# Window attention and FFN on one core: the first batch's mask on PE, values paired on VectorE, loads and stores rearranged

## The chip, the cores and the metric

The kernel runs on one core of a Trainium2 chip. The metric is the device time in microseconds; the times of the kernel before are eight runs. A profiled execution of the same kernel gives the trace that the text reads. In its tables PE is TensorE's matmuls, PEld its weight loads, DVE is VectorE, ACT is ScalarE, POOL is GpSimd, and SP is SyncE, which issues most loads. L456 means line 456 of the kernel before.

## What is computed

Attention in a window, then a feed-forward block with two weight matrices (FFN). q, k and v are 8 batches x 8 heads x 576 positions x 64, float32; w_in is 512 x 2048, w_out 2048 x 512. The output is 4608 x 512.

```python
scores = scale * np.matmul(q, k.transpose(0, 1, 3, 2))       # scale = 1/8
mask = np.abs(pos[:, None] - pos[None, :]) <= 32
scores = np.where(mask, scores, -1000000000.0)
attn = exp(scores - max) / (sum + 1e-09)
attn_out = np.matmul(attn, v)
x = attn_out.transpose(0, 2, 1, 3).reshape(4608, 512)
h = x @ w_in
g = 0.5 * h * (1.0 + np.tanh(c * (h + 0.044715 * h * h * h)))
out = g @ w_out
```

## The kernel before

**Stages.** x is kept transposed in a ring of 1536 columns (xT). The FFN works in nine stages t of 512 tokens; beside stage t the kernel computes the attention of batch t + 1, whose result the next stages need. Batch 0 has no stage before it: its attention and the first FFN product make up the head of the kernel, written out step by step at L596 to L707. From stage 1 on the second product is a seven-product scheme on 256-wide blocks (`WINO`, `ffn_out`, L534), whose sums of gelu blocks VectorE forms in `sums` (L491), after every fourth gelu.

**Attention of a batch.** The heads go in four pairs (groups 0 to 3); group 4 holds the last queries of all pairs (the tail queries, 128 to 143 in the kernel's order for batch 0). `score` (L349) puts 64x64 matmuls of keys and queries into PSUM, ScalarE takes exp (L370), `mask` (L373) multiplies by a 0/1 band on VectorE (L376), and `weigh` (L379) multiplies by the values and by ones, for the sums. `invert` (L405) forms 1/sum on ScalarE and `spread` (L412) writes the product to xT on VectorE. Scores of keys far from the window aren't computed; the band removes what is left over in the blocks. For `weigh` the value blocks are needed a second time, shifted by half a block: `pair_v` (L179) makes two copies within V. Batches 0, 1 and 2 use VectorE for that; for batches 3 to 7 the copies are two DMAs issued by SP at the end of the stage before (L796).

**Batch 0 and 1** come through SP as float32 (`load_early`, L126): queries and keys in quarters of two heads (L136), tail queries and keys into one tile tr (L149, L150), values head by head (L145). They are cast to float16 by VectorE or GpSimd (`cast_early`, L262; `cast_tails`, L277; `cast_v`, L271) and transposed on PE against an identity (`trans_pair`, L290; `trans_tails`, L282); VectorE copies the transposes from PSUM to QT and KT (L300, L301). Later batches are transposed by DMA on SP (`cast_and_turn`, L313), with tail queries and tail keys last (KL, L336), and their values are loaded by GpSimd's queue (`load_v`, L172).

**Weights.** w_in comes in four quarters of 1 MB, only the first in two halves (L215 to L217), and w_out in four quarters; each is cast chunk by chunk (`cast_w`, L199). Five staging buffers of 1 MB are shared by batch 0's values, w_in, batch 1's values and w_out, in that order.

**Order in the head.** Each engine runs its instructions in the order written. SP: q, k of pair 0; tail queries; tail keys; the other pairs; values; w_in; then batch 1's q and k, w_out, batch 1's values. PE: turn pair 0, tails, then for each pair scores, turn of the next pair, weighing, with idle matmuls between (`spin`, L223); then FFN products in pieces of 128 columns (`ffn_in`, L436). Ahead of pieces 12 to 15 PE transposes a pair of batch 1 (`TURN_0`, L52). `PLAN_0` (L53) sets where in the second product the attention of batch 1 runs, together with group 4 of batch 0.

**Stores.** `store` (L506) writes 128 rows of the output by as many DMAs as the order of the rows needs: each of the four residues j of a token within four is a run of its own. The last stage uses SP and ACT in turn, the others GpSimd.

Of the kernel before, what the change touches and what calls it, by code (L numbers as in the profile page):

```python
# [60 lines left out]
RING = 1536  # L61


@with_exitstack
def kernel(
# [44 lines left out]

    idn = const.tile([128, 128], FP16, name="idn")
    full = const.tile([128, 4, 56], FP16, name="full")
# [13 lines left out]
    def load_early(b):  # L126
# [21 lines left out]
        def tails():  # L148
            nc.sync.dma_start(tr[0:64, :, :], q[b, :, 512:576, :].rearrange("h s d -> s h d"))  # L149
            nc.sync.dma_start(tr[64:128, :, :], k[b, :, 512:576, :].rearrange("h s d -> s h d"))  # L150
# [48 lines left out]
    def cast_w(w, dst, on_dve=2, cs=range(4), on_act=()):  # L199
        for c in cs:  # L200
            (nc.scalar.copy if c in on_act else nc.vector.tensor_copy if c < on_dve else nc.gpsimd.tensor_copy)(  # L201
                dst[:, c, :], w[:, c, :])
# [3 lines left out]
    tails()  # L206
# [8 lines left out]
    wi = [load_w_in(0, stage_w(), 0, 2)]  # L215
    load_w_in(0, wi[0], 2, 4)
    wi[1:] = [load_w_in(i, stage_w()) for i in range(1, 4)]  # L217

# [4 lines left out]
    def spin(n, width, pair=None):  # L223
        ps = psS.tile([128, 2, 512], FP32, name="spin2", tag=f"S{pair}")[:, 0, :] if pair is not None else \
            psO.tile([128, 512], FP32, name="spin", tag="O")
        for _ in range(n):
# [7 lines left out]
                            base=0, pattern=[[1, 4], [4, 56]], channel_multiplier=-1)  # L234
    nc.gpsimd.affine_select(out=full, in_=full, compare_op=ALU.is_ge, fill=0.0,
                            base=64, pattern=[[-1, 4], [-4, 56]], channel_multiplier=1)
# [3 lines left out]
    def blocks(r, p0, n, pp0, w):  # L240
        nc.vector.tensor_copy(
            band[r, :, p0:p0 + n * w].rearrange("k j (n p) -> k j n p", n=n),
            full[r, :, pp0:pp0 + w].rearrange("k j (o p) -> k j o p", o=1).broadcast_to([64, 4, n, w]))

    even, odd = slice(0, 64), slice(64, 128)
    blocks(even, 0, 1, 8, 24)
    blocks(odd, 0, 1, 8, 40)
    blocks(even, 24, 3, 0, 32)
    blocks(odd, 40, 2, 16, 32)
    blocks(odd, 104, 1, 16, 40)  # L250
    blocks(even, 120, 1, 0, 24)
    nc.vector.memset(ones, 1.0)

# [23 lines left out]
    def cast_tails(b, eng):  # L277
        t16 = hp.tile([128, H, 64], FP16, name="t16", tag="t16")
        eng.tensor_copy(t16, raws[b][2])
        halfs[b].append(t16)  # L280

    def trans_tails(b, pt):  # L282
        t16 = halfs[b][2]
        for pr in range(NPAIR):
            nc.tensor.transpose(pt[:, pr, :], t16[:, 2 * pr:2 * pr + 2, :], idn)
        nc.vector.tensor_copy(KLs[b % 2], pt[:, 0:4, 64:128])
        nc.vector.tensor_copy(QTs[b][:, :, :, 128:144],
                              pt[:, 0:4, 0:64].rearrange("d r (p j) -> d r j p", j=4))
# [10 lines left out]
    def trans_out(b, pr, pt):  # L299
        nc.vector.tensor_copy(QTs[b][:, pr, :, 0:128], pt[:, 0:4, :])  # L300
        nc.vector.tensor_copy(  # L301
            KTs[b % 2][:, pr, :].rearrange("d (p j) -> d p j", j=4),
            pt[:, 4:8, :].rearrange("d j p -> d p j"))
# [45 lines left out]
    def score(b, g, pair):  # L349
        m, prs, steps, slots, q0, n = work_of(b, g)  # L350
        ps = psS.tile([128, 2, 512], FP32, name="ps_s", tag=f"S{pair}")
        for r, pr in enumerate(prs):
            for step in steps:
                for half, piece in enumerate(step):
# [3 lines left out]
                    for h in range(2):  # L358
# [6 lines left out]
                            QTs[b][r0:r0 + 64, pr, :, p0:p1], start=True, stop=True)  # L365
# [138 lines left out]
    turn_about = [nc.sync, nc.scalar]  # L504

    def store(t, t4, yo, cols=slice(0, 512), eng=None):  # L506
        m = 0
        while m < 128:
# [4 lines left out]
            if t == NT - 1 and eng is None:  # L513
                turn_about.reverse()
            (eng or turn_about[0] if t == NT - 1 else eng or nc.gpsimd).dma_start(  # L515
                out_v[b, j, q0 + p:q0 + p + e, cols], yo[m:m + e, cols])
            m += e

    later, unpaired = [], []
# [14 lines left out]
    def ffn_out(t, i):  # L534
# [37 lines left out]
        elif n == 4:  # L572
            if not end:
                nc.vector.tensor_tensor(C22, py, U3, op=ALU.add)
            else:
                for x, part in enumerate((py[:, 0, :], pys["apart"][:, 0:256])):
                    nc.vector.tensor_tensor(C22[:, x, :], part, U3[:, x, :], op=ALU.add)
                    store(t, 2 + x, yo[:, 2 + x, :], right)
        elif n == 5:
            nc.vector.tensor_tensor(C21, py, M1, op=ALU.add)  # L580
            for x in range(2):
                store(t, 2 + x, yo[:, 2 + x, :], left if end else slice(0, 512))

    def ffn_last(t):
        py = pys[0].rearrange("p (b c) -> p b c", b=2)
        yo, right = wino["yo"], slice(256, 512)
        for x in range(2):
# [4 lines left out]
            else:  # L592
                store(t, x, yo[:, x, :], right, nc.scalar if x else nc.sync)
# [3 lines left out]
    cast_early(0, 0, (nc.vector, nc.gpsimd))  # L597
    trans_pair(0, 0, bank16(0))
    cast_tails(0, nc.vector)
    spin(3, 512)  # L600
    trans_tails(0, bank16(1))
    both = (nc.gpsimd, nc.gpsimd)
    cast_early(0, 1, both)
    cast_early(0, 2, both)
    cast_v(0, 0)
    cast_early(0, 3, both)
    cast_v(0, 1)
    cast_v(0, 2)
    cast_v(0, 3)
    cast_w(wi[0], w_in16[:, :, 0:512], 0, (0, 1))  # L610
    cast_w(wi[0], w_in16[:, :, 0:512], 0, (2, 3))


# [5 lines left out]
    def turn(g):  # L619
        pt = bank16(0)  # L620
        trans_pair(0, g, pt, now=False)
        return pt

    def weighed(g):
        o, d = weigh(0, g, other=(g % 2 == 0))
# [7 lines left out]
    spin(2, 512, 1)  # L633
    pt = turn(1)
    trans_out(0, 1, pt)
    mask(0, 0)
    spin(4, 512, 1)
    score(0, 1, 1)
    pt = turn(2)
    trans_out(0, 2, pt)  # L640
    cast_vt(0)
    mask(0, 1)
    spin(4, 512, 0)
    score(0, 2, 0)
    paired(0)
    spin(3, 512, 1)
    weighed(0)
    mask(0, 2)
    pt = turn(3)
    trans_out(0, 3, pt)  # L650
    spread(0, 0, *ods[0])
    spin(4, 512, 1)
    score(0, 3, 1)
    paired(1)
    spin(2, 512, 0)
    weighed(1)
    paired(2)
    mask(0, 3)
    weighed(2)
    spread(0, 1, *ods[1])  # L660
    ffn_in(0, 0, 0, 2)
    paired(3)
# [165 lines left out]
```

The softmax here doesn't subtract the row's maximum and nothing guards it: scores larger than these inputs give would overflow.

## Time and profile before

| what | value |
|---|---|
| median of 8 runs | 302.89 us (302.18 to 305.96) |
| profiled execution | 302.18 us, span 300.5 us |
| busy in the span | PE 288.6, DVE 194.2, ACT 186.8, POOL 104.9, PEld 180.8 us |
| granted TensorE clock | 1.00 |
| q1, the hardware queue of SP | 84233 packets, 39.66 MB |
| q0, the software queue of POOL | 31776 packets, 11.41 MB |

The time outside of the span is 1.68 us. A page of the profile shows the span in 40 slices of 7.5 us, with the busy share of each engine in tenths. The DMA share is the mean over 16 engines. The timeline has one line for each instruction or run of instructions: start, length, engine, line, operation, result and input, and in brackets how long the engine had been idle before and what ended that. A "q" behind an engine's name (SPq, ACTq) is its queue of issues, not work.

### The profile page before, as it was taken

The numbers are of one execution on the slowest core, as the hardware profiler recorded it, in microseconds if no ns is written. First come the engines' busy times: TensorE is split into PE (matmuls) and PEld (weight loads), VectorE is DVE, ScalarE is ACT, GpSimd is POOL, SyncE is SP. The second block draws the span as 40 slices with busy tenths as digits, with TensorE's granted clock in tenths as the row PEclk, the third lists the DMA queues.
The fourth block names the chain that finished last, engine by engine and source line by source line (L and its number), as shares of the span: only waits on it lengthen the run. The fifth ranks groups of instructions, "written<-read, shape, count | busy, mean of one in ns | idle before, by whom it ended". The sixth has DMA issues, their size and how long they took to land.

```text
span 300.5 us, 7135 instructions
## 1 busy us (share of the span) xinstructions
PE 288.6 (96%) x2886; PEld 180.8 (60%) x2886; DVE 194.2 (65%) x429; ACT 186.8 (62%) x287; POOL 104.9 (35%) x160
## 2 busy tenths in 40 slices
PE   7879999999999999999999999999999999999993
PEld 2443544445784488448854885488547854784582
DVE  4783678879968486947694769466956634443442
ACT  1566586577765796669566956695669567606500
POOL 3655466266009300940094008500800070025000
PEclk9999999999999999999999999999999999999999
DMA  6999999999998999799979986999590041004013
GB/s 186 255 337 377 368 310 247 277 251 173 229 201 183 146 227 206 172 142 225 205 183 166 244 180 144 180 231 198 88 211 11 0 105 37 3 22 117 2 48 93
DMA packets 116831, 52.44 MB, mean 175 GB/s; under 512 B 97519, under 2 KB 109551, under 8 KB 116798
## 3 DMA queue, kind: packets, MB, share of 16 engines
q1 hardware_dynamic: 84233, 39.66, 59.9%
q0 software_dynamic: 31776, 11.41, 33.3%
q10 hardware_dynamic: 789, 0.92, 1.0%
q8 instruction: 22, 0.36, 0.6%
q14 instruction: 11, 0.09, 0.1%
HBM read 36.70 MB, written 9.44 MB: 154 GB/s over the span
## 4 chain that ended last, share of the span: by engine, by line
PE 73%; SPq 9%; DMA 8%; DVE 5%; POOL 1%; issue 1%; ACT 0%; DVEq 0%
PE mm L551 31%; PE mm L456 19%; PE ph L456 15%; DMA wst<-in_moe_w_out_dram 3%; SPq L145 3%; DMA wst<-in_moe_w_in_dram 3%; PE ps_s L360 2%; SPq L167 2%; PE ps_d L389 2%; DMA qt<-in_q_dram 2%; DVE s L499 2%; PE ps_o L395 2%; SPq L136 2%; POOL w_in L201 1%; DVE t L489 1%
## 5 line engine op out<-in xcount | busy, mean ns | idle before, releaser
L456 PEld LDWEIGHTS <-w_in 128*128 128x128 f16 x576 | 56.0, 98 | 67.3 <-POOL w_in L201 2.7
L515 POOL DMA_DIRECT2D out_dram<-y x77 | 46.4, 610 | 113.0 <-DVE y L580 99.3
L456 PE MATMUL mm<-xT,w_in 128*128 128x512 f16 x320 | 78.4, 379 | 0.8 <-POOL w_in L201 0.8
L464 ACT ACTIVATE gT<-mm 128x512 f16<-128x512 f32 x80 | 47.6, 599 | 45.5 <-PE mm L456 44.7
L456 PE MATMUL ph<-xT,w_in 128*128 128x512 f16 x256 | 64.6, 379 | 0.5 <-POOL w_in L201 0.3
L499 DVE TENSOR_TENSOR s<-gT 128x512 f16<-128x512 f16 x64 | 26.8, 419 | 41.7 <-ACT gT L464 41.7
L551 PEld LDWEIGHTS <-s 128*128 128x128 f16 x512 | 49.6, 98 | 5.9
L370 ACT ACTIVATE pe<-ps_s 128x960 f16<-128x960 f32 (+1 forms) x32 | 30.5, 976 | 23.6 <-PE ps_s L360 23.5
L551 PE MATMUL mm<-t,s 128*128 128x256 f16 x376 | 44.7, 273 | 0.0
L464 ACT ACTIVATE gT<-ph 128x512 f16<-128x512 f32 x64 | 36.0, 603 | 10.1 <-PE ph L456 10.0
L551 PEld LDWEIGHTS <-gT 128*128 128x128 f16 x384 | 36.0, 98 | 6.6
L551 PE MATMUL mm<-w_out,gT 128*128 128x256 f16 x256 | 32.8, 273 | 0.5 <-DVE y L562 0.5
L409 ACT ACTIVATE lt<-lt 128x480 f32<-128x480 f32 (+3 forms) x40 | 23.5, 587 | 1.3
L90 ACT ACT_TABLE_LOAD x17 | 21.8, 1283 | 1.1 <-PEq L812 0.8
L408 ACT ACTIVATE lt<-ps_d 128x480 f32<-128x480 f32 (+2 forms) x29 | 16.1, 554 | 10.1 <-PE ps_d L389 6.2
L175 POOL DMA_DIRECT2D V<-in_v_dram x24 | 22.0, 938 | 1.0 <-PE mm L456 0.6
L376 DVE TENSOR_TENSOR pe<-pe,band 128x960 f16<-128x960 f16 (+1 forms) x32 | 20.6, 659 | 1.4 <-ACT pe L370 1.4
L395 PEld LDWEIGHTS <-V 128*64 128x64 f16 x520 | 14.5, 111 | 4.3 <-DVE V L183 0.8
L551 PE MATMUL mm<-t,gT 128*128 128x256 f16 x128 | 16.3, 273 | 0.0
L360 PEld LDWEIGHTS <-KT 64*64 64x64 f16 x576 | 9.6, 106 | 8.1 <-issue 5.7
L551 PE MATMUL mm<-w_out,s 128*128 128x256 f16 x120 | 14.4, 273 | 0.0
L499 DVE TENSOR_TENSOR s<-s,gT 128x512 f16<-128x512 f16 x32 | 13.6, 425 | 1.1
(90 smaller groups left out, 306.3 us busy)
## 6 DMA issues: line engine op xcount, KB each, us to landing
kr<-in_k_dram SPq DMA_DIRECT2D x32, 256.0 KB, 8.6
qr<-in_q_dram SPq DMA_DIRECT2D x6, 1024.0 KB, 8.2
wst<-in_moe_w_in_dram SPq DMA_DIRECT2D x3, 1024.0 KB
wst<-in_moe_w_out_dram SPq DMA_DIRECT2D x3, 1024.0 KB, 11.9
V<-in_v_dram POOLq DMA_DIRECT2D x24, 128.0 KB, 7.9
qr<-in_q_dram SPq DMA_DIRECT2D x8, 256.0 KB, 10.1
vr<-in_v_dram SPq DMA_DIRECT2D x16, 128.0 KB, 4.5
V<-V SPq DMA_DIRECT2D x5, 256.0 KB
```

The source lines that it names most:

```text
L90: nc.scalar.add_instruction(mybir.InstLoadActFuncSet(name=nc.get_next_instruction_name(), act_func_set_id=which, ins=[], outs=[]))
L175: nc.gpsimd.dma_start(V[:, c, :, :], v[b, :, 128 * c:128 * c + 128, :].rearrange("h p d -> p h d"))
L370: nc.scalar.activation(pe, ps[:, :, 0:w], AF.Exp, scale=SCALE)
L376: nc.vector.tensor_tensor(pe, pe, m.rearrange("k (o j) p -> k o j p", o=1).broadcast_to(list(pe.shape)), op=ALU.mult)
L395: nc.tensor.matmul(o[64 * h:64 * h + 64, cols].rearrange("d (j p) -> d j p", j=4)[:, :, p0 - q0:p1 - q0], Vs[b % 2][:, slot, 2 * pr + h, : ...
L408: nc.scalar.activation(lt[:, 0:n], d[:, 0:n], AF.Ln)
L409: nc.scalar.activation(lt[:, 0:n], lt[:, 0:n], AF.Exp, scale=-1.0)
L456: nc.tensor.matmul(ph, w_in16[:, dc, fc * 128:fc * 128 + 128], xT[:, dc, t * 512 % RING:t * 512 % RING + 512], start=(dc == 0), stop=(dc = ...
L464: nc.scalar.activation(gTs[t][:, fc, :], phs[fc], AF.Gelu_apprx_tanh)
L499: nc.vector.tensor_tensor(dst, x, y, op=op)
L515: (eng or turn_about[0] if t == NT - 1 else eng or nc.gpsimd).dma_start(out_v[b, j, q0 + p:q0 + p + e, cols], yo[m:m + e, cols])
L551: nc.tensor.matmul(pys["apart"][:, 0:256] if apart else py[:, blk, :], lhsT, wino[w][:, f, :], start=(new and i % (8 if one else 16) == 0) ...
```

## The change

- **Mask of batch 0's groups 0 to 3.** A bias, 0 inside the band and -30000 outside, is put into PSUM ahead of the scores by four matmuls of 64x64 tiles over 512 columns in each group (an identity times the bias); the scores are added to it, and the four `mask` steps go away. The bias tiles lie in columns of xT that are not used yet. They are built from `full`, which has 64 columns instead of 56, by one VectorE operation, three VectorE copies and three ScalarE copies. The band is built after the last `spread` of batch 0.
- **Tail queries of batch 0** are loaded behind w_in's second quarter instead of among the first loads, cast by GpSimd and turned on PE ahead of FFN piece 12, with pair 0 of batch 1. Tail keys stay early.
- **w_in** comes in eight halves. Of quarter 1 VectorE casts chunks 0 and 2 and GpSimd 1 and 3 (before: all on GpSimd). The FFN's first pieces go chunk by chunk over four pieces, then over two.
- **Head of batch 0.** Queries of pairs 1 and 2 are cast by VectorE (before: GpSimd). QT of pairs 0 and 2 is copied by ScalarE. Casts, idle matmuls and weighing change their places.
- **Values.** `pair_v` of batches 3 to 7 runs on VectorE after FFN piece 8 of their stage. GpSimd's `load_v` of the stages first copies one element of KL.
- **Stores.** Adjacent residues j whose rows are whole are joined into one DMA; in the last stage the two queues alternate within each call of `store`.

```diff
-        def tails():
-            nc.sync.dma_start(tr[0:64, :, :], q[b, :, 512:576, :].rearrange("h s d -> s h d"))
-            nc.sync.dma_start(tr[64:128, :, :], k[b, :, 512:576, :].rearrange("h s d -> s h d"))
+        def tails(which="qk"):
+            if "q" in which:
+                nc.sync.dma_start(tr[0:64, :, :], q[b, :, 512:576, :].rearrange("h s d -> s h d"))
+            if "k" in which:
+                nc.sync.dma_start(tr[64:128, :, :], k[b, :, 512:576, :].rearrange("h s d -> s h d"))
...
 qk(0)
-tails()
+tails("k")
...
-    wi = [load_w_in(0, stage_w(), 0, 2)]
-    load_w_in(0, wi[0], 2, 4)
-    wi[1:] = [load_w_in(i, stage_w()) for i in range(1, 4)]
+    wi = []
+    for i in range(4):
+        wi.append(load_w_in(i, stage_w(), 0, 2))
+        load_w_in(i, wi[i], 2, 4)
+        if i == 1:
+            tails("q")
...
+    bias = [xT[:, i, RING - 512:RING].rearrange("k (j p) -> k j p", j=4) for i in range(2)]
+    low = xT[:, 2, RING - 512:RING - 256].rearrange("k (j v) -> k j v", j=4)
+    nc.vector.tensor_scalar(low, full, scalar1=-1.0, scalar2=-LOW, op0=ALU.add, op1=ALU.mult)
+    for r in (even, odd):
+        blocks(nc.vector.tensor_copy, bias[0], low, r, (0, 1, 24, 8), (24, 3, 32, 0), (120, 1, 8, 0))
+        blocks(nc.scalar.copy, bias[1], low, r, (0, 1, 40, -8), (40, 2, 32, 0), (104, 1, 24, 0))
...
     def score(b, g, pair):
+        added = b == 0 and g < 4
+        if added:
+            for half in range(2):
+                for h in range(2):
+                    r0 = 64 * h
+                    nc.tensor.matmul(ps[64 * half:64 * half + 64, h, :], idn[r0:r0 + 64, r0:r0 + 64],
+                                     bias[half][r0:r0 + 64, :, :], start=True, stop=False,
+                                     skip_group_check=True)
...
-                            QTs[b][r0:r0 + 64, pr, :, p0:p1], start=True, stop=True)
+                            QTs[b][r0:r0 + 64, pr, :, p0:p1], start=not added, stop=True,
+                            skip_group_check=added)
...
+            nj = 1 if p else max(1, min(4 - j, (128 - m) // n))
+            eng = engs[i % len(engs)] if engs else nc.gpsimd
+            if nj > 1:
+                e = nj * n
+                eng.dma_start(out_v[b, j:j + nj, q0:q0 + n, cols], yo[m:m + e, cols])
...
-                    store(t, 2 + x, yo[:, 2 + x, :], right)
+                    store(t, 2 + x, yo[:, 2 + x, :], right, nc.sync, nc.scalar)
...
-                store(t, x, yo[:, x, :], right, nc.scalar if x else nc.sync)
+                store(t, x, yo[:, x, :], right, *((nc.scalar, nc.sync) if x else (nc.sync,)))
...
+    split = (nc.vector, nc.gpsimd)
...
+    cast_early(0, 1, split)
...
     score(0, 3, 1)
     paired(1)
+    spread(0, 0, *ods[0])
     weighed(1)
     paired(2)
+    spin(2, 512, 0)
+    weighed(2, pair=1)
+    spread(0, 1, *ods[1])
     paired(3)
+    weighed(3)
+    spread(0, 2, *ods[2])
+    spin(3, 512, 0)
+    for dc in range(3):
+        for fc in range(4):
+            ffn_in(0, fc, dc, dc + 1)
     spread(0, 3, *ods[3])
+    band_out()
+    cast_w(wi[1], w_in16[:, :, 512:1024], (0, 2))
+    for dc in range(3):
+        for fc in (4, 5):
+            ffn_in(0, fc, dc, dc + 1)
...
+            if pr == 0:
+                cast_tails(0, nc.gpsimd, even)
...
+            if pr == 0:
+                trans_tails(0, pt[:, 1], even)
         ffn_in(0, fc)
...
+                if t > 1 and fc == 8 and att:
+                    pair_v(b, nc.vector.tensor_copy)
...
                     if t and g < 0 and b + 1 < B:
+                        nc.gpsimd.tensor_copy(after, KLs[b % 2][:, 3, 0:1])
                         load_v(b + 1)
-                        unpaired.append(b + 1)
...
-        if unpaired:
-            pair_v(unpaired.pop(), nc.sync.dma_start)
```

## The prediction

> **What bounds the kernel now.** I read the forty slices of the page first, then a table by stage, then the chain of waits over the first 80 us, then the timeline around each edit. The slices:
>
> ```profile
> PE   7879999999999999999999999999999999999993
> DMA  6999999999998999799979986999590041004013
> ```
>
> PE is busy from end to end, but a busy PE is not one that never waits. In the stages after 82 us its starts follow each other without a gap: eight 128x512 matmuls take 1.73 us, 0.216 each, and one stage lasts 30.42 us (121.59 to 152.00). The diff adds no instruction to PE there and takes none away. So only three places can move the time: the head up to about 80 us, a new wait in the stages, and the last 5 us. The table by stage for the head (after the times come PE, PEld, DVE, ACT, POOL busy, granted clock, DMA share, GB/s):
>
> ```profile
> 2.00:6.00 4.00, 4.00 (x17) 1.85 (x16) 1.99 (x9) 0.09 (x1) 1.06 (x4) 1.00 0.79 231
> 10.00:18.00 8.00, 6.97 (x107) 3.43 (x107) 7.00 (x14) 4.43 (x6) 3.96 (x7) 1.00 1.18 241
> 18.00:26.00 8.00, 6.27 (x71) 2.93 (x70) 4.43 (x9) 5.22 (x8) 5.29 (x9) 1.00 1.04 391
> 32.00:40.00 8.00, 7.38 (x87) 4.27 (x86) 5.85 (x13) 4.21 (x7) 3.32 (x5) 1.00 1.06 379
> 40.00:58.00 18.00, 17.78 (x189) 8.60 (x188) 15.59 (x28) 12.18 (x20) 9.50 (x12) 1.00 1.08 264
> ```
>
> From 6 us on the DMA engines are never free (share 1.04 and more); only in the first stage are they starved (0.79), because SP can't issue fast enough. The chain of waits agrees: it runs from transfer to transfer.
>
> ```profile
> 15.37 8.24 DMA wst<-in_moe_w_in_dram
> 23.67 1.73 POOL w_in L201 x3
> ...
> 31.08 9.87 DMA wst<-in_moe_w_out_dram
> 41.00 1.86 POOL w_out L201 x2
> ...
> 57.98 6.19 DMA qt<-in_q_dram
> ```
>
> So the head is paced by the bytes to be loaded, and the change moves the same bytes in nearly the same order. That is the core of my forecast.
>
> **The head, step by step.** *Tail queries later.* The issue at L149 takes 0.74 us of SP while SP is the limit, so everything behind it, up to the second quarter of w_in, can start up to 0.74 us sooner. The 128 KB then come back behind that quarter, at the rate for rows of 64 floats (241 GB/s in 10 to 18): 0.54 us. For all later loads 0.74 - 0.54 = 0.20 us stays. Bounds: 0, if transfer only changes its place, and 0.74; I take 0.2.
>
> *Weights in halves.* Three more issues on SP of 0.5 us each (L192); SP is held back by the engines there (3.73 us for five issues), so they cost nothing. A first half lands about 1.3 us before the second: the two halves of quarter 0 were cast from 19.63 and 20.96, 512 KB in 1.33 us, 394 GB/s; the whole quarters came at 23.67 and 26.35, 391 GB/s. Halves are not slower here. The Trainium skill (DMA: Bandwidth & Descriptors, Bandwidth) speaks against halves: it asks for at least 1 MiB in a DMA, and its fit charges about 2 us to each. By it three more DMAs would cost up to 6 us (an estimate from that page) if they stood in line; the two rates of the trace say that they overlap, and the measurement decides.
>
> *Mask on PE.* It removes four mask products on VectorE (L376, 0.68 each) from between exp and the weighing. It adds 16 matmuls of 64x64 tiles over 512 columns. The trace has none; the nearest row gives 0.216 for 512 columns, so a group of four costs 0.22 if the tiles run beside each other and 0.86 if not. They stand in front of the scores, where PE now waits for KT (at 11.01, 13.09 and 16.98 the weight load stood 0.74 before each). I take 0; the worst is 0.12 a group. The bias needs one VectorE product, three VectorE copies (0.22 each, like the six of L241) and three on ScalarE (at most 0.62 each, the 64x512 copy at 12.51). VectorE has until qr lands at 3.61, ScalarE until 8.95. The six copies of band, 1.34 us, move behind the last spread; VectorE idles 2.75 us there, and the next user of band is at 41.67.
>
> *What this gives PE.* With casts split between VectorE and GpSimd, QT copies on ScalarE and no mask, I get the last spread at 21.3 instead of 22.91, and the first FFN matmul at 19.7 instead of 20.30 (w_in lands by 0.5 to 0.7 sooner). Fourteen matmuls are done before 25.45 today, so 24 are done at 25.45 + 10 x 0.216 = 27.6. In the new order the halves of quarter 1 land near 21.8 and 23.1, their casts end near 24, and 24 matmuls are done at about 25.6. PE leads by 2.0 us. But then it meets this:
>
> ```profile
> 31.04 0.43 DVE L264 CAST k<-kr 128x512 f16<-128x512 f32 x1 [0.33 <-DMA kr<-in_k_dram]
> 31.13 1.36 POOL L264 CAST q<-qr 128x512 f16<-128x512 f32 x2
> 32.91 0.39 PE L293 MATMUL pt<-idn,q 128*128 128x128 f16 x4
> 33.36 1.03 PE L456 MATMUL ph<-xT,w_in 128*128 128x512 f16 x4
> ```
>
> Ahead of the FFN's piece 12 PE must transpose batch 1's first pair, whose keys land at 31.04, and, new, the tail queries. GpSimd casts those after its two q casts: 31.13 + 1.36 = 32.49, plus 0.60 (the 64x512 cast at 52.71) is 33.1, plus 0.2 for the transposes: piece 12 begins at 33.3, against 33.36 today. PE has caught up with the loads, and its lead is gone. Further on it would not help either: w_out's first quarter is cast until 39.9 and PE waits 0.37 for it now; the last values of batch 1 land at 52.15 and are used at 53.93 without slack; batch 2's tail queries land at 64.17 and hold VectorE. Each comes sooner by the 0.2 alone. Head: **-0.2 us** (0 to -0.74).
>
> **The stages.** Values are paired on VectorE in five stages (t 2 to 6), instead of two DMAs on SP at each stage's end. The rows: 64x1024 took 0.42 and 64x768 took 0.42, so twice the width takes 1.7 us. The place is between the second and third sums:
>
> ```profile
> 99.23 0.42 DVE L499 TENSOR_TENSOR s<-gT,s 128x512 f16<-128x512 f16 x1
> 101.55 0.43 DVE L499 TENSOR_TENSOR s<-gT 128x512 f16<-128x512 f16 x1 [1.90 <-ACT gT L464]
> ```
>
> 1.7 fits into 1.90. Behind it another 1.90 is free before the last sums, so up to 3.6 us of copies reach no PE instruction. Such copies at L182 took 0.29 with GpSimd idle and 0.58 beside its casts. The Trainium skill (Advanced Engine Details and Errata, Mode Summary) says why: VectorE's second port is shared with GpSimd, and the two block each other. By the doubled row it would be 3.4 us, and still nothing on PE.
>
> GpSimd's value loads now wait for KL, through a 1-element copy (0.19, like L727). They go from 96.88 to about 106; behind them on GpSimd stand only the stores, at 120.22. They are used a stage later. Stages: **0**; without this cover 1 us on VectorE costs up to 5 us.
>
> **The end.**
>
> ```profile
> 294.53 0.66 SPq L515 DMA_DIRECT2D out_dram<-y  x2
> ...
> 295.56 0.42 DVE L589 TENSOR_TENSOR y<-py,y 128x256 f32<-128x256 f32 x1 [0.45 <-PE py L551]
> ...
> 296.01 0.80 ACTq L515 DMA_DIRECT2D out_dram<-y  x2
> 296.92 0.36 SPq L515 DMA_DIRECT2D out_dram<-y  x1
> ```
>
> The last data is ready at 295.98, yet SP's last store is issued at 296.92. From 294.53 SP issues six stores, 0.48 apart ((296.92 - 294.53) / 5). The five stores of the last row block become two, so the left halves need two issues on each queue instead of four and three; with two for the third part and one for the last, SP has five. Its last starts at 294.53 + 4 x 0.48 = 296.45: **-0.5 us**. Bounds: 0, if the landing of the bytes sets the end, and -0.9, if the store follows its data at once. Joined stores in other stages lie on GpSimd, off the path.
>
> **Sum.** -0.2 + 0 - 0.5 = -0.7. The profiled execution took 302.18 (span 300.5), so 301.5. It is the fastest of the runs shown; their median is 302.89, which is what I predict from: **302.2 us**, with 301.2 to 302.9 from the bounds alone.
>
> **Rivals.** *A, PE's lead survives.* For it: the 2.0 us of lead at 25.6, and the idle time that PE still has to give, 1.73 in 18 to 26 and 0.62 in 32 to 40 by the table. It needs batch 1's keys and w_out's first quarter earlier too, that is, transfers that run better once SP issues sooner. Against it: the share of 1.04 to 1.08, and 380 to 390 GB/s held over 18 us. Price: 302.2 - 2.0 = 300.2; half of it is as likely. Chance 0.24.
>
> *B, slower: values and the next batch's loads collide.* The value loads (576 KB) move into the stretch where SP loads the next q and k (104.33 to 116.79), and the pairing DMAs (448 KB) leave it. The last load, kt, lands 5.4 us after its issue, near 122.2; VectorE wants it at 125.7 and works in order. Up to 3.5 us of delay is free; after that the sums shift, and once their gaps (0.9, 0.2, 1.9) are used up PE waits in five stages. 0.5 us too late in each costs 2.5: 304.7. Against it: 576 - 448 = 128 KB more is about 0.5 us. Chance 0.14.
>
> *C, nothing but the forecast's terms, or not even those*: if neither issue nor store was on the path, 302.9. It lies inside the forecast's case, which has 0.62.
>
> **How the numbers follow.** A measurement of this kernel can tell about 0.5%, 1.5 us, from no change: 301.4 to 304.4. Faster: A, 0.24, and 0.05 from the forecast's lower edge. Slower: B, 0.14, less 0.02 for a small excess. The rest, 0.59, is within. The range takes the forecast's case with 0.9 for the scatter of the runs (302.18 to 303.54 but for one) on the upper side, and reaches down to 300.0 for most of A; B is left out.
>
> **What the new profile would show.** Right: 24 FFN matmuls done before 26; PE waiting near 31 to 33 for the transposes of tail queries; its piece 12 at 33.1 to 33.4; w_out cast to 39.7; stages of 30.4; the sums' third gap filled with 1.7 of V copies; the last store issued near 296.4 - 0.2. Wrong: piece 12 before 32 and w_out's cast end before 39 (A); VectorE waiting for kt, or a stage over 30.6 (B); scores later than 11.0, 13.1 and 17.0, which would mean that the bias matmuls are not hidden; a store end that follows the transfers.

## The result, and the profile after

The changed kernel takes **305.44 us** (median of 12 runs, 304.7 to 307.67) against 303.09 us for the kernel before (33 runs on the same chip): ratio **1.0084**, 95% interval 1.0063 to 1.0105. It is slower; 302.2 had been forecast, with 303.8 as the upper end. The ratios here are those of undisturbed runs, without those over 1.5% above the fastest of the same kernel: in joined_and_wait that leaves out five of nine, so the table has its median too, and in no_wait_for_KL too few stay for a ratio, so the table has its times. Line numbers are now those of the changed kernel, whose L480, L383, L346, L542 were L456, L360, L331, L515.

The profiled execution took 303.61 us, span 301.9, so it is faster than all timed runs. It is 1.43 us behind the profile of before. The timed runs' spans go from 301.8 to 305.7, with a median of 303.6, so most of what they take beyond the profile lies within the span. The time outside of the span is 1.7 to 2.0 us in nine of the twelve and 2.5 to 3.2 in three; in the runs of the kernels with the head of before, as far as their spans are on record, it is 1.8 at most. No run here explains this. The same two rows of its slices:

```profile
PE   8979699999999999999999999999999999999994
DMA  6999999999997999698989996979593031004013
```

The fifth slice (30 to 37.5 us) has fallen from 9 to 6. The table by stage, in the columns of before, has the reason a little earlier:

```profile
10.00:18.00 8.00, 7.32 (x131) 3.83 (x129) 5.05 (x12) 5.26 (x8) 3.66 (x6) 1.00 1.17 285
18.00:26.00 8.00, 6.17 (x59) 3.12 (x59) 4.98 (x15) 4.65 (x8) 3.86 (x6) 1.00 1.04 286
32.00:40.00 8.00, 5.41 (x48) 3.08 (x46) 5.59 (x11) 2.24 (x5) 3.43 (x7) 1.00 1.07 374
```

From 18 to 26 us the DMA engines are as busy as before (share 1.04 in both) but move 286 GB/s instead of 391. In the last row PE has lost 1.97 us (7.38 to 5.41). The chain of waits again goes through loads, and through something new at its end, the transposes of batch 2's keys by DMA:

```profile
15.58 8.48 DMA wst<-in_moe_w_in_dram
...
24.08 9.14 DMA qr<-in_q_dram
...
33.29 11.84 DMA wst<-in_moe_w_out_dram
...
66.90 8.54 DMA KT<-k
```

To see where time goes, I cut each profile in three: until stage 1 begins (its first FFN product), the length of stage 1, and from the beginning of stage 2 to the end of the span. Each row is one execution, whose own time stands in the third column; all in us:

| kernel | ratio, 95% interval | profiled time | first cast of w_out | stage 1 begins | its length | from stage 2 on |
|---|---|---|---|---|---|---|
| before | 1 | 302.18 | 38.26 | 58.75 | 31.61 | 210.14 |
| changed | 1.0084 [1.0063, 1.0105] | 303.61 | 39.72 | 60.47 | 31.63 | 209.80 |
| head_only | 1.0107 [1.0065, 1.0149] | 303.77 | 39.94 | 60.68 | 30.83 | 210.59 |
| stages_only | 1.0027 [0.9996, 1.0058] | 306.39 | 37.88 | 58.82 | 35.87 | 210.01 |
| end_only | 0.9969 [0.9939, 0.9999] | 303.98 | 38.33 | 59.99 | 32.32 | 209.99 |
| before_tails_late | 1.0026 [1.0001, 1.0051] | 302.75 | 38.47 | 59.72 | 31.19 | 210.09 |
| before_halves | 1.0018 [0.9981, 1.0056] | 302.45 | 38.31 | 58.88 | 32.31 | 209.51 |
| tails_early | 1.0048 [1.0016, 1.0079] | 306.38 | 39.41 | 60.02 | 34.75 | 209.93 |
| w_in_whole | 1.0045 [1.0018, 1.0072] | 308.15 | 40.87 | 62.21 | 34.59 | 209.60 |
| loads_as_before | 1.0025 [1.0000, 1.0050] | 302.82 | 38.65 | 59.49 | 31.32 | 210.29 |
| tails_own_bank | 1.0063 [1.0035, 1.0092] | 306.59 | 39.75 | 60.55 | 34.19 | 210.06 |
| no_values_2 | 1.0077 [1.0044, 1.0109] | 307.58 | 41.40 | 63.54 | 31.07 | 209.69 |
| before_joined | 1.0502 [1.0462, 1.0541] | 317.86 | 38.21 | 58.73 | 31.95 | 225.52 |
| joined_and_wait | 1.0146 [1.0090, 1.0201]; median of all nine 311.05 us | 311.05 | 37.66 | 58.17 | 30.82 | 220.31 |
| no_wait_for_KL | 317.02 to 324.85 us | 324.85 | 40.26 | 62.40 | 31.75 | 228.85 |
| pairs_by_dma | 1.0639 [1.0598, 1.0679] | 327.47 | 40.04 | 61.79 | 31.38 | 232.63 |
| stages_values_early | 1.0105 [1.0049, 1.0160] | 306.41 | 37.96 | 58.79 | 35.41 | 210.49 |
| loads_values_early | 1.0155 [1.0113, 1.0197] | 308.08 | 39.48 | 60.40 | 36.16 | 209.80 |
| stages_free_in_1 | 1.0011 [0.9984, 1.0038] | 304.16 | 39.11 | 60.53 | 32.15 | 209.76 |
| changed_free_in_1 | 1.0059 [1.0028, 1.0089] | 305.87 | 40.13 | 62.34 | 31.94 | 209.86 |

In the first two rows the change costs +1.72 until stage 1, +0.02 in it, -0.34 after it. But single executions scatter. Seven kernels have the head of before (before, before_joined, joined_and_wait, stages_only, stages_values_early, stages_free_in_1, end_only): they first cast w_out at 37.66 to 39.11 (mean 38.20) and begin stage 1 at 58.17 to 60.53 (59.11). Six have the changed head (changed, head_only, no_values_2, changed_free_in_1, no_wait_for_KL, pairs_by_dma): 39.72 to 41.40 (40.25) and 60.47 to 63.54 (61.87). So the changed head is some 2 us late at w_out and 2.8 at stage 1, while a difference of 1.5 us between two single rows says little. The length of stage 1 scatters too, and is taken up below.

### The profile page after: what moved, and what is told of

The parts are those of the page before. It is cut to its first block, busy times and chain, and to the rows that moved or that the text cites. A ratio compares the mean times of both kernels' runs of the same rounds, so it can differ in the third digit from the quotient of the medians.

```text
span 301.9 us, 7164 instructions
## 1 busy us (share of the span) xinstructions
PE 289.4 (96%) x2909; PEld 181.5 (60%) x2909; DVE 200.6 (66%) x444; ACT 189.3 (63%) x295; POOL 95.1 (32%) x147
## 4 chain that ended last, share of the span: by engine, by line
PE 69%; DMA 17%; SPq 7%; DVE 2%; issue 1%; POOL 1%; ACT 1%; DVEq 0%
PE mm L578 31%; PE mm L480 17%; PE ph L480 13%; DMA KT<-k 5%; DMA wst<-in_moe_w_out_dram 4%; DMA qr<-in_q_dram 3%; DMA wst<-in_moe_w_in_dram 3%; PE ps_s L383 3%; PE ps_d L413 2%; DMA kr<-in_k_dram 2%; PE ps_o L419 2%; SPq L169 2%; SPq L145 2%; SPq L136 1%; SPq L152 1%
## 5 line engine op out<-in xcount | busy, mean ns | idle before, releaser
L480 PEld LDWEIGHTS <-w_in 128*128 128x128 f16 x576 | 56.0, 98 | 65.6 <-POOL w_in L203 0.3
L480 PE MATMUL mm<-xT,w_in 128*128 128x512 f16 x320 | 78.2, 379 | 0.0
L480 PE MATMUL ph<-xT,w_in 128*128 128x512 f16 x256 | 64.2, 379 | 0.0
L542 POOL DMA_DIRECT2D out_dram<-y x55 | 32.9, 607 | 90.8 <-DVE y L607 82.1
L400 DVE TENSOR_TENSOR pe<-pe,band 128x960 f16<-128x960 f16 x28 | 17.7, 650 | 2.9 <-ACT pe L394 2.9
L801 POOL COPY after<-KL 128x1 f16<-128x1 f16 x5 | 1.9, 387 | 52.6 <-DMA KL<-kt 52.6
L383 PE MATMUL ps_s<-QT,KT 64*64 64x128 f16 (+3 forms) x576 | 13.1, 216 | 1.5 <-DMA KT<-k 0.8
```

The source lines that it names most:

```text
L383: nc.tensor.matmul(ps[64 * half:64 * half + 64, h, 4 * n * r:4 * n * r + 4 * n].rearrange("k (j p) -> k j p", j=4)[:, :, p0 - q0:p1 - q0], ...
L400: nc.vector.tensor_tensor(pe, pe, m.rearrange("k (o j) p -> k o j p", o=1).broadcast_to(list(pe.shape)), op=ALU.mult)
L480: nc.tensor.matmul(ph, w_in16[:, dc, fc * 128:fc * 128 + 128], xT[:, dc, t * 512 % RING:t * 512 % RING + 512], start=(dc == 0), stop=(dc = ...
L542: eng.dma_start(out_v[b, j, q0 + p:q0 + p + e, cols], yo[m:m + e, cols])
```

## The experiments

**Head or stages?** Two kernels split the change.

*head_only* is the changed kernel with `store`, the pairs by DMA and the value loads of before; *stages_only* is the kernel before with these three from the change, that is:

```diff
+            nj = 1 if p else max(1, min(4 - j, (128 - m) // n))
...
+                if t > 1 and fc == 8 and att:
+                    pair_v(b, nc.vector.tensor_copy)
...
+                        nc.gpsimd.tensor_copy(after, KLs[b % 2][:, 3, 0:1])
                         load_v(b + 1)
-                        unpaired.append(b + 1)
```

> The changed kernel's whole head (mask on PE, tail queries later, weights in halves, the new order), with the stages and stores of the kernel before. If the head makes the slowdown: 305.5 to 306, ratio 1.010, that is the changed kernel's and the 0.5 us of the end more; batch 1's first keys at 32.5 us and a wait of PE for KT near 75 to 79 us of 0.6 or more. If the stages make it: 303, ratio 1.000.

> The kernel before, with its whole head (up to 60 us), and only what the change does from the stages on: values paired on VectorE, value loads of GpSimd behind the copy of KL, joined stores, the last stage's stores shared by two queues. If the slowdown lies in the head and first stage alone, this is free of it and keeps the 0.5 us of the end: 302.5, ratio 0.998, stages of 30.4 us, and the wait for KT at 78 us stays at 0.5 or less. If the joined stores still cost something behind the wait for KL (value loads at 107 us beside SP's loads of the next batch), some stage is over 30.6 us and the time is above 304.

The head alone costs no less than the whole change, 1.0107. The stages alone aren't the gain that I expected, 1.0027; the profile shows a long stage 1, taken up below. The stores of the last stage, which stages_only includes, are worth 0.9969 by themselves (end_only). So the rest of the stages costs about 0.0058, 1.8 us (0.4 to 3.1 by the two intervals).

**What the tail queries and halves cost.** *before_tails_late* and *before_halves* put one part each into the kernel before; *tails_early* and *w_in_whole* take one part each out of the changed kernel; *loads_as_before* takes out both.

```diff
before_tails_late (casts and transposes of the tail queries follow, as in the change)
-    tails()
+    tails("k")
...
+    tails("q")
before_halves
-    wi[1:] = [load_w_in(i, stage_w()) for i in range(1, 4)]
+    for i in range(4):
+        wi.append(load_w_in(i, stage_w(), 0, 2))
+        load_w_in(i, wi[i], 2, 4)
tails_early
-    tails("k")
+    tails()
w_in_whole (loads_as_before: tails() at the start, and no tails("q"))
+    wi = [load_w_in(0, stage_w(), 0, 2)]
+    load_w_in(0, wi[0], 2, 4)
+    wi.append(load_w_in(1, stage_w()))
+    tails("q")
+    wi += [load_w_in(i, stage_w()) for i in range(2, 4)]
```

> The kernel before, with one part of the change alone: batch 0's tail queries loaded behind w_in's second quarter, cast by GpSimd and turned ahead of FFN piece 12 in the shared PSUM tile. Theory 1: the slower loads and the wait show here too: 1.4 to 2.0 us over the kernel before, 304.5 to 305.1. Theory 2: within 0.3 of 303.1. Theory 3: within 0.3 of 303.1.

> The kernel before with one part of the change alone: all of w_in in halves. Theory 1: the starved stretch and loads that come 1 to 1.3 us later show here too; 1.0 to 2.5 us over the kernel before. Theory 2: within 0.4 us of the kernel before.

> The changed kernel with the tail queries loaded, cast and turned at the start again, as before; all else as changed. Theory 1: w_in lands without the gap at 21 to 24 us, piece 12 begins at 33.4 or sooner, and the 1.7 us of the head are back: 303.4 to 303.9, or near 302.5 if the faster store end shows as well. Theory 2: the time stays at or above 304.8, with a mean granted clock near 0.994. Theory 3: within 0.3 of 305.4.

> The changed kernel with quarters 1 to 3 of w_in loaded whole, as before; all else as changed, tail queries late too. Theory 1 (three more and smaller DMAs starve the DMA engines between 15 and 21 us, so every later load comes 1.2 us later, batch 2's KT too, and PE's wait for KT in stage 1 then lowers its granted clock): no slice under 300 GB/s in 15 to 21 us, batch 1's first keys cast at 31.2 to 31.5 instead of 32.5, w_out's first quarter at 38.3 to 38.6 instead of 39.7, no wait for KT over 0.5 us in stage 1, and a time of 302.8 to 303.6 where the kernel before has 303.3. Theory 2 (the tail queries' wait at piece 12 and the order of the head are the cause, the halves are not): no gain beyond 0.5 us, 304.8 or more.

> The changed kernel with the load queue of the kernel before: tail queries first and quarters 1 to 3 of w_in whole. Mask on PE, the new order of the head and all of the stages stay. Each of the two alone left 1.0048 and 1.0045. If their costs add (later loads by 1.2 to 1.5 us from both), this has w_in's last half cast from 29.6, w_out's first quarter from 38.3, a wait for KT in stage 1 under 0.6 us, and takes 302.5 to 303, ratio 0.998 to 1.000. If the new order of the head's work (casts on GpSimd, PE) holds the loads back by itself, the loads are still late by 1 us or more and the ratio stays near 1.005.

Three rows of the stretch in which the tail queries land in the changed kernel: before, changed, and changed with the tail queries early.

```profile
18.00:24.00 6.00, 4.74 (x66) 2.43 (x64) 4.43 (x9) 5.05 (x8) 3.34 (x6) 1.00 1.04 393
```

```profile
18.00:24.00 6.00, 4.17 (x50) 2.19 (x50) 4.56 (x14) 4.65 (x8) 3.00 (x5) 1.00 1.04 258
```

```profile
18.00:24.00 6.00, 4.64 (x52) 2.29 (x51) 5.05 (x15) 4.55 (x7) 3.20 (x6) 1.00 1.02 365
```

With the same share of 1.02 to 1.04, 258 GB/s becomes 365 when the tail queries are gone from there. This holds over all 20 profiles: from 21 to 24 us the nine kernels with late tail queries move 211 to 338 GB/s, the other eleven 379 to 408.

In time, the tail queries alone cost 0.0026 and the halves alone 0.0018, less than the 1.4 us and 1.0 us that theory 1 of each expected. Taken out of the changed kernel, either brings back about 0.004 (1.0048 and 1.0045), with intervals that overlap that of the changed kernel; tails_early (304.32 us) lies between what its theories expected, and so does loads_as_before (303.53). Both together bring back 0.0059, 1.8 us (0.8 to 2.8), and here the intervals are apart: 1.0025 [1.0000, 1.0050] against 1.0084 [1.0063, 1.0105]. What is left, 1.0025, is as much as stages_only has with the whole head of before (1.0027). So the order of the loads is what costs the head its time; how much of it is the tail queries and how much the halves, these runs don't tell, and they show no clear cost of the other parts of the head. The three parts alone, 0.0026, 0.0018 and 0.0025, add up to 0.0069, which the intervals don't tell from 0.0084. The expectation that w_in_whole would bring the loads forward failed: w_out is first cast at 40.87, in the range of the changed head.

**Does the wait ahead of FFN piece 12 matter?** In the changed kernel's timeline:

```profile
32.48 0.58 DVE L277 CAST k<-kr 128x512 f16<-128x512 f32 x1 [2.18 <-DMA kr<-in_k_dram]
32.83 0.40 PE L308 MATMUL pt<-idn,q 128*128 128x128 f16 x4 [0.16 <-POOL q L277]
33.82 0.60 POOL L293 CAST t<-tr 64x512 f16<-64x512 f32 x1
33.99 0.71 DVE L277 CAST k<-kr 128x512 f16<-128x512 f32 x1 [0.94 <-DMA kr<-in_k_dram]
34.96 0.68 DVE L316 COPY KT<-pt 128x512 f16<-128x512 f16 x1
35.69 0.27 PE L298 MATMUL pt<-idn,t 64*128 64x64 f16 x4 [2.18 <-DVE KT L316]
35.90 1.04 PE L480 MATMUL ph<-xT,w_in 128*128 128x512 f16 x4
```

The tail queries are cast at 34.42, but PE turns them at 35.69: they go into the other half of the PSUM tile in which pair 0 lies, and wait for VectorE's copy out of it (L316), which stands behind a cast that waits for the next keys. *tails_own_bank* gives them another tile:

```diff
-                trans_tails(0, pt[:, 1], even)
+                trans_tails(0, psO.tile([128, 8, 128], FP16, name="pt", tag="O"), even)
```

> The changed kernel, with batch 0's tail queries turned into a PSUM tile of their own instead of the second half of the tile that pair 0 of batch 1 uses. Theory 1 (the moved tail queries cost the head 1.7 us: their 128 KB slow the loads behind them, and their transposes wait for the KT copy from the shared PSUM tile): the wait of 2.2 us before the transposes falls to about 1.0 (end of GpSimd's cast), FFN piece 12 begins near 34.8 instead of 35.9, and the time falls by 0.6 to 1.1, to 304.4 to 304.9. Theory 2 (PE is granted a lower clock in the timed runs; the head matters little): within 0.3 of 305.4. Theory 3 (values paired on VectorE hurt the stages): within 0.3 of 305.4.

There piece 12 begins at 34.75 instead of 35.90, yet stage 1 begins at 60.55 (60.47 in the changed kernel). The ratio falls by 0.0021, 0.6 us, and the intervals overlap. The wait is real; whether it costs time these runs don't tell. Here PE later waits 0.37 for w_out at 41.45, where the changed kernel has no such wait, so a part of it only changes its place.

**The stages: three parts that need each other.** Each of these runs takes one away, or puts one into the kernel before.

```diff
no_wait_for_KL (from the changed kernel)
-                        nc.gpsimd.tensor_copy(after, KLs[b % 2][:, 3, 0:1])
pairs_by_dma (this too, and)
-                if t > 1 and fc == 8 and att:
-                    pair_v(b, nc.vector.tensor_copy)
+        if unpaired:
+            pair_v(unpaired.pop(), nc.sync.dma_start)
before_joined (from the kernel before; joined_and_wait adds the copy of KL to it)
+            nj = 1 if p or t == NT - 1 else max(1, min(4 - j, (128 - m) // n))
```

> The changed kernel with the values of batches 3 to 7 paired by SP's DMAs and GpSimd's value loads not waiting for KL, as before; all else as changed. Theory 1: within 0.3 of 305.4, since the stages of the profile last 30.42 us in both kernels. Theory 2: within 0.3 too. Theory 3: below 304.5.

> The changed kernel without the one-element copy of KL ahead of GpSimd's value loads, so that these start when the stores are issued; values are still paired on VectorE. Theory A (value loads that run beside the DMA transposes make KT late; the run with pairing by DMA lost 18 us that way): KT late in several stages, PE waits of 2 us and more, clock below 0.98, a time over 310. Theory B (it was the pairing DMAs on SP, ahead of the next transposes, that made KT late there): within 1 us of the changed kernel, 304.5 to 306.5.

> The kernel before with the stores of stages 0 to 7 joined as in the change, and nothing else. GpSimd then gets to its value loads earlier by about 0.6 us for each store saved. Theory A (earlier value loads alone push KT late): PE waits for KT in several stages, 305 or more. Theory B (joined stores lie off the path): within 0.4 us of the kernel before.

> The kernel before with joined stores, which alone took 1.050, and with one thing more: the one-element copy of KL that holds back GpSimd's value loads. If the early value loads are what pushes the KT transposes back, the copy removes all of it: 303 to 304, ratio 1.000, no wait for KT over 0.6 us from stage 2 on. If the joined transfers themselves, or their time, harm the transposes, the ratio stays above 1.03.

All three theories missed pairs_by_dma, which took 323.32 us. For no_wait_for_KL and before_joined theory A was right. Joined stores alone cost 5%. In the kernel before eleven stores hold GpSimd until batch 3's transposes are under way (the "q" lines are issues, TRANSPOSE lines those of the DMA transposes):

```profile
89.80 7.09 POOL L515 DMA_DIRECT2D out_dram<-y  x11 [14.39 <-DVE y L580]
92.72 3.38 SPq L324 DMA_TRANSPOSE QT<-q  x1
96.20 5.50 SPq L331 DMA_TRANSPOSE KT<-k  x2
96.88 3.62 POOL L175 DMA_DIRECT2D V<-in_v_dram  x4
```

In before_joined eight issues do, and the value loads go in ahead of KT:

```profile
93.03 5.91 SPq L324 DMA_TRANSPOSE QT<-q  x1
...
95.16 4.02 POOL L175 DMA_DIRECT2D V<-in_v_dram  x4
99.03 6.35 SPq L331 DMA_TRANSPOSE KT<-k  x2
...
107.98 1.02 PE L360 MATMUL ps_s<-QT,KT 64*64 64x96 f16 x32 [2.89 <-DMA KT<-k]
```

The transposes take 12.3 us to issue instead of 8.9 and PE waits 2.89 for KT. In the changed kernel the values wait until KL is there:

```profile
100.08 3.07 SPq L346 DMA_TRANSPOSE KT<-k  x2
...
106.96 0.25 POOL L801 COPY after<-KL 128x1 f16<-128x1 f16 x1 [10.39 <-DMA KL<-kt]
107.51 3.58 POOL L177 DMA_DIRECT2D V<-in_v_dram  x4 [0.30 <-PE ps_o L419]
```

The copy alone isn't enough (joined_and_wait, 1.0146, between its two expectations, with 311.05 us as the median of all nine): values that land later push the pairing DMAs to 90.17 (88.07 in before_joined), right ahead of the transposes, and QT takes 7.93 us to issue. With the pairs on VectorE as well, the stages are back at 210. That value loads issued early make KT late is shown by no_wait_for_KL, which differs from the changed kernel by the one line: 317 to 325 us instead of 305. The theory that joined transfers harm by themselves falls, since the changed kernel has them.

**The long stage 1.** Stage 1 takes 30.8 to 32.3 us, or 34.2 to 36.2. In the long form PE waits over 1.7 us for KT near 77 us. I thought of batch 2's value loads, issued from 64 us. *no_values_2* leaves them out; *stages_values_early* and *loads_values_early* issue them sooner on each of two heads.

```diff
                        load_qk(2)
+                        load_v(2)
...
-                    nc.gpsimd.tensor_copy(after, gTs[1][:, column(1, 2), 0:1])
-                    load_v(2)
```

> The changed kernel without the value loads of batch 2 on GpSimd (576 KB from about 64 us, beside the transposes of batch 2); batch 2 is weighed with what stands in the buffer. If these loads are what makes the KT transposes of stage 1 late (their issue takes 5.65 us in the changed kernel, against 4.25 before), the issue takes 4 us or less, no wait for KT is left at 75 us, and the time falls to 303 to 303.5 (ratio 1.000), the rest being the later loads of the head and the stage's start that is 1.7 us late. If the transposes are late only because they start late, the wait and the ratio of about 1.008 stay.

> The kernel before's head and the change's stages (alone 1.0027, with a wait for KT at 77 us in its profile), with one thing more: batch 2's value loads are issued some 8 us sooner, at the end of GpSimd's casts, so that they land before the transposes. If they are what stands beside the transposes, the wait for KT at 77 us goes and the 0.5 us of the end is kept: 302 to 302.5, ratio 0.997. If moving them holds up batch 2's keys instead (bytes are bytes), the transposes start up to 2 us later and the time is 304 or more.

> The changed kernel with the load queue of the kernel before (1.0025) and batch 2's value loads issued some 8 us sooner, at the end of GpSimd's casts. Same question on the changed head: 302 to 302.5, ratio 0.997 if the loads beside the transposes were the rest; 304 or more if batch 2's keys come later by it.

Without the loads KT's issue takes 4.03 us and the wait is gone, but the ratio stays at 1.0077. In its profile the head is later than in any other (stage 1 begins at 63.54); that the head is the whole rest is argued, not shown. Earlier loads are worse, 1.0105 [1.0049, 1.0160] and 1.0155 [1.0113, 1.0197], with stage 1 at 35.41 and 36.16: KT took 6.60 us to issue in the former and QT 7.29 in the latter. So some us sooner is no better place.

Last, the wait for KL in stage 1 itself, taken away there alone, on the stages and on the changed kernel:

```diff
-                        nc.gpsimd.tensor_copy(after, KLs[b % 2][:, 3, 0:1])
+                        if t > 1:
+                            nc.gpsimd.tensor_copy(after, KLs[b % 2][:, 3, 0:1])
```

> The kernel before's head and the change's stages (alone 1.0027), but in stage 1 the value loads don't wait for KL, as in the kernel before; from stage 2 on they do. Six of the eight profiles with the wait in all stages, joined stores and pairs on VectorE have a stage 1 of 34 us and more; none of the others has. If it is the wait in stage 1 that makes KT late there, stage 1 takes 31 to 32.5 us and the time is 302.0 to 302.5, ratio 0.997. If it is chance, or the earlier stores, a wait for KT of over 1.5 us can stay, and the ratio is about 1.003.

> The changed kernel, but in stage 1 the value loads don't wait for KL. If the wait in stage 1 adds to the slowdown: ratio 1.005 or less, stage 1 of 31 to 32 us; what stays is the later head (stage 1 begins 1.7 us later). If not: 1.008 as the changed kernel, or more, if the loads of batch 3's values beside the transposes make KT later still.

1.0011 [0.9984, 1.0038] and 1.0059 [1.0028, 1.0089], stage 1 of 32.15 and 31.94. Both ratios are lower than with the wait (1.0027, 1.0084), but the intervals overlap. Over all profiles the long form came in 6 of 10 with a wait for KL in stage 1 and in none of 10 without. So the copy in stage 1 goes with the long form. Why is open: the loads held back there are batch 3's, and they come after KT.

**The end.** *end_only* is the kernel before with the last stage's stores of the change.

```diff
+            nj = 1 if p or t < NT - 1 else max(1, min(4 - j, (128 - m) // n))
...
-                    store(t, 2 + x, yo[:, 2 + x, :], right)
+                    store(t, 2 + x, yo[:, 2 + x, :], right, nc.sync, nc.scalar)
```

> The kernel before with nothing but the last stage's stores of the change: joined, and shared by the queues of SP and ScalarE. Prediction's step for the end: 0.5 us less, ratio 0.998, with the span ending 3.9 us behind the last VectorE operation instead of 4.5. If the end of the transfers sets the span, nothing: 1.000.

0.9969 [0.9939, 0.9999]: the only version here whose whole interval lies below 1, if barely.

## Why the prediction was wrong

Two terms of the sum failed. The loads of the head were put at -0.2 us (tail queries -0.2, halves 0), and measured +1.8 (0.8 to 2.8). The stages were put at 0, and measured about +1.8 (0.4 to 3.1). The end was put at -0.5, and measured -0.9 (-1.8 to 0.0). Together these are 2.7 us, where the whole change measured 0.0084, 2.5 us.

*Mask on PE: right.* The four bias matmuls took 0.41 us together, and scores began at 8.26, 10.78, 13.53 and 16.52 (before: 8.26, 11.01, 13.09, 16.98). The one at 13.53 is later than the forecast's limit of 13.1, but it waits 0.56 for the copy of KT, and the bias matmuls ahead of it were done before.

*PE's lead of 2.0 us: wrong.* The last spread of groups 0 to 3 began at 21.56 (forecast 21.3), but the first FFN matmul ran at 22.04 (forecast 19.7; before 20.30):

```profile
22.04 0.59 PE L480 MATMUL mm<-xT,w_in 128*128 128x512 f16 x2
...
26.35 1.89 PE L480 MATMUL ph<-xT,w_in 128*128 128x512 f16 x8
```

From there 24 matmuls, 0.216 apart, are done at 27.2 (forecast 25.6; before 27.6), so the lead was 0.4 us. Ahead of the first PE waits 0.97 for the copy to xT and 0.86 for the copy of V, and runs idle matmuls until 22.04, although the first chunks of w_in are cast from 18.33. So it is the order of work on PE and VectorE that took the lead, and rival A fell before the loads could take it.

*Halves, 0: right as a single part* (1.0018, 0.9981 to 1.0056); beside late tail queries they may cost more, as said above. The Trainium skill (DMA: Bandwidth & Descriptors, Bandwidth) gives its rule of 1 MiB, and its fit of 2 us a DMA, from DMAs issued by GpSimd. These loads are SP's: 1.0018 does not bear the rule out, but leaves room for up to 1.7 us.

*Tail queries, "-0.2 us (0 to -0.74)": the step that failed.* SP did run ahead: w_in's first chunk is cast at 18.33 instead of 19.63. But 0.54 us for the 128 KB was mis-sized. From 21 to 24 us the engines moved 223, 195 and 217 GB/s, 635 KB, where before they moved 403, 399 and 393, 1195 KB. Without the 128 KB that is 507 KB of other loads, so by this estimate the tail queries took (1195 - 507) / 398 = 1.7 us of them. The same sum gives 1.1 in head_only (294 GB/s) and 1.3 in before_tails_late (267). The 241 GB/s that I used came from 10 to 18 us, where longer rows were loaded alongside. Early, the same rows cost little, because the engines were starved there (share 0.79 in 2 to 6). By 28 us 279 GB/s over 27 us have moved 7533 KB against 7965; the missing 432 KB are 1.1 us at 382 GB/s (kernels with the head of before: 285 to 303 GB/s, with the changed head: 254 to 280), and the second half of w_in's last quarter is cast at 31.06 instead of 29.57. That my worse bound was "0, if transfer only changes its place" is the real fault: a move from a stretch with spare DMA time to one without can be a loss, and here it was one. That short rows are the reason is argued; no run loads the same bytes in longer rows. The Trainium skill (DMA: Bandwidth & Descriptors, Specifications) sets 512 B as the least for line rate; these rows have 256 B, and the trace agrees in sign, with 258 GB/s against 393.

*"Each comes sooner by the 0.2 alone": wrong sign by the same step.* Paced by loads is right: w_out's first cast is 1.46 later and stage 1 begins 1.72 later. With the order of the loads put back (loads_as_before) w_out's first cast is at 38.65, in the range of the old head (39.48 in loads_values_early, which loads the same until then).

*Piece 12 at 33.3: wrong.* It began at 35.90, for the shared PSUM tile; the row of before at 35.94, where a transpose waits 0.25 for the KT copy, shows this kind of wait, and I didn't read it. What it cost is not clear of noise (0.6 us).

*Stages, 0: right from stage 2 on, by cover that I mis-saw, and wrong in stage 1.* The pair copies took less than the forecast 1.7, at the forecast place:

```profile
101.40 0.69 DVE L184 COPY V<-V 64x2048 f16<-64x2048 f16 x1
102.11 0.55 DVE L185 COPY V<-V 64x1536 f16<-64x1536 f16 x1
```

The value loads went to 107.51 ("about 106"), and a stage from stage 2 on is still 30.42. But in stage 1, where batch 2's transposes run, PE can wait for KT, and the stage then takes 34.2 to 36.2 instead of 30.8 to 32.3; the forecast had no term for it. And "joined stores lie on GpSimd, off the path" is false: their issue time decides when values are loaded, and so when KT is there. Alone they cost 5%; the KL copy that I counted as a cost without effect is what pays for them. Rival B had a collision of values with SP's loads in the stages; it named the wrong place (kt, VectorE), and it didn't happen there.

*The end, -0.5: sign right, size doubtful.* The last store now follows its data at once:

```profile
297.55 0.42 DVE L616 TENSOR_TENSOR y<-py,y 128x256 f32<-128x256 f32 x1 [0.45 <-PE py L578]
298.00 0.33 ACTq L542 DMA_DIRECT2D out_dram<-y  x1
```

The span ends 3.93 us behind the last VectorE operation, against 4.52. Over more profiles it is 3.9 to 4.5 with old stores (six, mean 4.31) and 3.9 to 4.3 with new (fourteen, mean 4.1): 0.2 rather than 0.5. The times of end_only allow 0 to 1.8.

## What to carry to other kernels

A DMA share near 1 says that the engines are occupied, not that bytes flow: read GB/s beside it, and price a moved transfer by what it displaces where it goes, not by its own rate. An engine that only issues DMAs sets their order against other queues: before making it faster, look at what it will issue next and what that runs into. Parts of a change that protect one another must be priced together, and one at a time only to find which protects which.

## What the runs showed that I had not expected

- DMA transposes are slowed by other transfers beside them. QT's and KT's issues of one batch (3 to 6) take 8.4 to 9.9 us together in the changed kernel and 9.2 to 13.1 in no_wait_for_KL. QT's alone takes 2.45 to 3.38 for batches 3 to 5 in the kernel before, and 6.49 to 7.93 in joined_and_wait, where the pairing DMAs end right ahead of it. KT's alone is no measure: it takes 3.07 to 6.90 within the changed kernel.
- A wait of PE is paid twice. In stages_values_early PE waits for KT, and the granted clock (third column from the end) falls with it:

```profile
76.50 0.69 PE L360 MATMUL ps_s<-QT,KT 64*64 64x96 f16 x32 [3.29 <-DMA KT<-k]
```

```profile
75.00:80.00 5.00, 3.50 (x52) 2.52 (x53) 1.20 (x4) 2.74 (x4) 1.15 (x3) 0.69 0.53 115
80.00:85.00 5.00, 5.00 (x82) 4.11 (x80) 4.07 (x8) 2.18 (x4) 3.28 (x4) 0.97 1.28 271
```

  In tails_own_bank 1.96 us of waiting are followed by 0.84 and 0.82 in the same two stretches, while in stages_free_in_1 a wait of 1.58 left 1.00. All 20 profiles fit: the six with a long stage 1 have a wait for KT of 1.75 to 3.74 there and then a stretch at 0.66 to 0.82, and the fourteen others have 1.58 at most and 1.00 from 70 to 85 us. So the two forms of stage 1 go with the clock: in tails_own_bank the wait costs 1.96 and the clock, by an estimate from these stretches, another 1.7 (5 x 0.16 + 5 x 0.18). The Trainium skill (TensorE: Matmul & The Clock Gate, Part 1) has the clock halve after an idle window of about 3.4 us; the 3.29 is near it, and 1.96 is well below.
